# Pairing the 64-row score tiles of an attention + rational-MLP kernel, and moving one PSUM copy from ACT to DVE

## The chip, the cores and the metric

One core of a Trainium2 chip. The metric is the device time of one execution in microseconds (us). The kernel before took 747.16 us, the median of 3 runs (745.7 to 747.44). The engines are called as in the profile: PE is TensorE (its matrix multiplies; PEld is its weight loads), DVE is VectorE, ACT is ScalarE, POOL is GpSimd, SP is SyncE. SBUF is the working memory, PSUM the memory that PE writes its results to.

## The reference

Attention over q, k, v of shape (4, 12, 448, 64), fp32, with capped scores, and a two-layer MLP with a rational activation on its result.

```python
scores = np.matmul(q, k.transpose(0, 1, 3, 2)) / np.sqrt(64)
scores = cap * np.tanh(scores / cap)
attn = np.exp(scores - np.max(scores, axis=-1, keepdims=True))
attn = attn / (np.sum(attn, axis=-1, keepdims=True) + 1e-09)
x = (attn @ v).transpose(0, 2, 1, 3).reshape(1792, 768)
h = x @ w_in                                    # w_in: 768 x 2048
P = a[0] + a[1]*h + a[2]*h**2 + a[3]*h**3
Q = 1.0 + abs(b[0])*abs(h) + abs(b[1])*h**2
out = (P / (Q + 1e-06)) @ w_out                 # w_out: 2048 x 768
```

## The kernel before

The program has two halves: attention (24 pairs of heads, p = 0 to 23), up to about 245 us of the profile, and the MLP. Products are made exact enough by splitting an fp32 operand into a high and a low part: each product is three matmuls (low·high, high·low, high·high).

**Scores (L360).** A pair of heads is worked on together. Its keys are cut into four tiles, n = 0 to 3. Tiles 0 to 2 have 128 keys of each of the two heads, and the head dimension is 64, so the array is used as two halves of 64 rows: head 0 on rows 0 to 63, head 1 on rows 64 to 127. Such a tile is six matmuls of 64 rows by 448 columns (L380), which run two at a time, and it fills both banks of one of the three PSUM buffers PS[0] to PS[2] (448 fp32 columns for each head). Tile 3 holds the last 64 keys of both heads in one product over all 128 rows: three matmuls (L285, `ps`), one bank. A "visit" below is a stretch of PE's order in which only 64-row score matmuls stand. The buffer of tile n of pair p is `(4p + n) % 3` (L365).

**Softmax (L384, L405).** ACT takes tanh in place in PSUM (L392) and exp from PSUM to SBUF (L409), which frees the buffer. DVE splits the result: a cast gives the high part (L416), a subtraction the low part (L417).

**P·V (L446).** For each of the two heads (j = 0, 1): nine matmuls of 66 columns (L285, `pv`) and one in fp32 for the tail (L459, shown as two), all into the one PSUM bank `pv`. Then ACT copies 65 rows x 448 columns of it to SBUF (L470) for either head, which frees the bank for the next head; small DMAs take the denominators and, for j = 1, the result into its place. The P·V of pair p - 1 stands among the score tiles of pair p (L564, L565).

**Preparation (L289).** Two pairs ahead, q and k are transposed on PE (L304 to L310) into `mi`; ACT makes the high parts (L318, L324), DVE the low ones (L319, L327). Pair 1 uses PS[1] and PS[2] for it instead of `mi` (L342 to L343). Besides, pairs 5 to 10 carry the conversion of six weight tiles from 64-bit words (L647 on ACT, L649 to L655 on DVE), the normalisation of finished pairs (L514 on DVE), and pairs 21 to 23 the first splits of x for the MLP (L525 on ACT, L526 on DVE), placed by `XSPLIT` as (pair counted from the end, n).

**What sets the order.** The kernel records every operation with an estimated cost, and a list scheduler (`Plan.flush`, L116) replays them on five engines and emits each engine's order. An engine takes, among what is ready, the operation that stands earliest in the program. The costs fix only the order; on the chip each engine runs its order strictly and waits for semaphores. A 64-row tile is one operation with the cost `SC_NS` = 760 ns (L55, L382). The order in the program is that of the loop at L553: for each pair and n, the scores, the softmax, then preparation, P·V, loads and the rest.

## Time and profile before

| What | Value |
|---|---|
| Median of 3 runs | 747.16 us (745.7 to 747.44) |
| The profiled execution | 744.5 us, of which the span (first to last instruction) is 742.7 us |
| PE busy | 711.1 us (96%) |
| DVE busy | 590.2 us (79%) |
| ACT busy | 529.3 us (71%) |
| POOL busy | 129.6 us (17%) |
| Mean granted clock of TensorE | 0.992 of full speed |

How to read it: "busy" is the time in which at least one instruction of the engine is under way. Matmuls are pipelined: a group's last matmul is still shown as running when the next group begins, so what a group costs PE is the distance from its start to the start of the next group. The same holds, by less, for DVE and ACT. Names such as `ps`, `pv`, `mi` are tiles without their buffer numbers, `arena_f` and `arena_r` the two large SBUF arrays that hold nearly everything.

### The profile page before, as it was taken

The numbers are of one execution on the slowest core, as the hardware profiler recorded it, in microseconds if no ns is written. First come the engines' busy times: TensorE is split into PE (matmuls) and PEld (weight loads), VectorE is DVE, ScalarE is ACT, GpSimd is POOL, SyncE is SP. The second block draws the span as 40 slices with busy tenths as digits, with TensorE's granted clock in tenths as the row PEclk, the third lists the DMA queues.
The fourth block names the chain that finished last, engine by engine and source line by source line (L and its number), as shares of the span: only waits on it lengthen the run. The fifth ranks groups of instructions, "written<-read, shape, count | busy, mean of one in ns | idle before, by whom it ended". The sixth has DMA issues, their size and how long they took to land.

```text
span 742.7 us, 10184 instructions
## 1 busy us (share of the span) xinstructions
PE 711.1 (96%) x3733; PEld 594.1 (80%) x3733; DVE 590.2 (79%) x720; ACT 529.3 (71%) x701; POOL 129.6 (17%) x193
## 2 busy tenths in 40 slices
PE   7999999999999999999799889899999999999996
PEld 4666656665656899989798889789999999999996
DVE  4879989998887689898677767779668878887863
ACT  6999989989898768877676777785674446444560
POOL 3222423422321000221222222120000000000030
PEclk9999999999999999999899999999999999999999
DMA  6668878556244345999899989795420121121065
GB/s 142 157 174 201 214 194 192 129 130 144 54 128 107 91 139 158 251 269 250 216 237 245 240 212 227 165 196 180 140 64 23 43 76 53 43 64 43 1 118 185
DMA packets 92252, 109.48 MB, mean 147 GB/s; under 512 B 50064, under 2 KB 69392, under 8 KB 92192
## 3 DMA queue, kind: packets, MB, share of 16 engines
q1 hardware_dynamic: 78272, 74.77, 34.5%
q0 software_dynamic: 13920, 33.96, 23.5%
q8 instruction: 31, 0.51, 0.3%
q14 instruction: 29, 0.24, 0.1%
HBM read 62.13 MB, written 18.17 MB: 108 GB/s over the span
## 4 chain that ended last, share of the span: by engine, by line
PE 59%; issue 17%; DMA 9%; DVE 6%; ACT 4%; POOL 4%; POOLq 0%; DVEq 0%; ACTq 0%
PE ps L285 20%; PE pv L285 10%; PE ps L751 9%; PE ps L380 5%; PE pv L751 5%; PE mi L751 4%; DMA arena_r<-X 4%; PE pv L459 4%; POOL arena_f L258 3%; DMA arena_f<-arena_f 2%; PE mi L310 1%; DMA arena_f<-dn 1%; ACT ps L392 1%; DMA dn<-arena_f 1%; PE mi L304 1%
## 5 line engine op out<-in xcount | busy, mean ns | idle before, releaser
L285 PE MATMUL ps<-arena_r 128*128 128x448 f32 x1224 | 274.7, 373 | 1.4 <-ACT arena_f L409 1.4
L285 PEld LDWEIGHTS ps<-arena_r 128*128 128x128 f32 x1224 | 229.6, 189 | 28.6 <-issue 5.0
L258 POOL DMA_DIRECT2D arena_f<-arena_f x112 | 79.5, 713 | 456.1 <-ACT arena_f L782 351.5
L751 PE MATMUL ps<-arena_r 128*128 128x384 f32 x672 | 129.7, 339 | 9.3 <-ACT arena_f L782 7.9
L751 PEld LDWEIGHTS ps<-arena_r 128*128 128x128 f32 x672 | 119.3, 190 | 12.8 <-ACT arena_f L782 9.9
L751 PE MATMUL pv<-arena_r 128*128 128x384 f32 x336 | 112.6, 338 | 6.9 <-DMA arena_r<-X 3.7
L751 PE MATMUL mi<-arena_r 128*128 128x384 f32 x336 | 112.7, 338 | 0.6 <-ACT arena_f L782 0.4
L285 PE MATMUL pv<-arena_r 128*66 128x448 f32 x432 | 100.2, 371 | 0.0
L409 ACT ACTIVATE arena_f<-ps,acap 128x896 f32<-128x896 f32 (+1 forms) x96 | 86.2, 920 | 0.4
L720 DVE SCALAR_TENSOR_TENSOR arena_f<-arena_f,bab 128x896 f32<-128x896 f32 x32 | 36.8, 1151 | 58.6 <-ACT arena_f L717 58.5
L285 PEld LDWEIGHTS pv<-arena_r 128*66 128x66 f32 x432 | 56.0, 136 | 31.5 <-issue 5.5
L392 ACT ACTIVATE ps<-ps 128x896 f32<-128x896 f32 (+1 forms) x96 | 76.1, 814 | 5.7 <-PE ps L380 5.2
L417 DVE TENSOR_TENSOR arena_r<-arena_f,arena_r 128x896 fp32r<-128x896 f32 x72 | 77.7, 1082 | 0.9
L751 PEld LDWEIGHTS pv<-arena_r 128*128 128x128 f32 x336 | 63.0, 188 | 10.0 <-ACT arena_f L782 4.9
L671 ACT ACTIVATE arena_r<-X 128x768 fp32r<-128x768 f32 x64 | 54.3, 848 | 20.1 <-DMA X<-w 6.1
L751 PEld LDWEIGHTS mi<-arena_r 128*128 128x128 f32 x336 | 63.1, 188 | 3.2 <-ACT arena_f L782 1.9
L728 ACT CAST arena_r<-arena_f 128x896 fp32r<-128x896 f32 x32 | 30.1, 939 | 46.9 <-DVE arena_f L727 46.9
L380 PE MATMUL ps<-arena_r 64*128 64x448 f32 x432 | 60.6, 392 | 2.1 <-DVE arena_r L319 1.3
L716 ACT ACTIVATE arena_f<-ps,b 128x896 f32<-128x896 f32 x32 | 32.3, 1010 | 40.5 <-PE ps L285 40.5
L380 PEld LDWEIGHTS ps<-arena_r 64*128 64x128 f32 x432 | 35.8, 184 | 28.7 <-issue 17.3
L416 DVE CAST arena_r<-arena_f 128x896 fp32r<-128x896 f32 x72 | 44.1, 618 | 11.2 <-ACT arena_f L409 10.8
L678 DVE SCALAR_TENSOR_TENSOR arena_r<-X,arena_r 128x768 fp32r<-128x768 f32 x48 | 45.7, 951 | 4.0 <-ACT arena_r L671 4.0
(92 smaller groups left out, 901.5 us busy)
## 6 DMA issues: line engine op xcount, KB each, us to landing
arena_f<-arena_f POOLq DMA_DIRECT2D x49, 384.0 KB, 6.9
X<-w SPq DMA_DIRECT2D x38, 384.0 KB, 3.1
arena_f<-in_moe_w_in_dram SPq DMA_DIRECT2D x16, 768.0 KB, 7.1
w<-X SPq DMA_DIRECT2D x32, 384.0 KB, 3.7
arena_f<-in_moe_w_out_dram SPq DMA_DIRECT2D x16, 768.0 KB, 7.8
arena_r<-X POOLq DMA_DIRECT2D x16, 384.0 KB, 8.5
arena_f<-in_q_dram SPq DMA_DIRECT2D x46, 112.0 KB, 4.0
out_dram<-arena_f SPq DMA_DIRECT2D x13, 384.0 KB, 2.3
```

The costliest lines, as they stand in the source:

```text
L258: self.op(eng, (625 if local else 450) if eng == SP else 1050, lambda: e.dma_start(out, in_, **accum), r, w, nbytes=nbytes, **kw)
L285: r = nc.tensor.matmul(out, st, mv, start=(first and y == 0), stop=(last and y == len(ops) - 1))
L380: m = nc.tensor.matmul(self.PS[i][:, j, 0:448], st[r], mv[r], start=y == 0, stop=y == 2)
L392: self.op(ACT, act_ns(448 * w, True), lambda: nc.scalar.activation(ps, ps, AF.Tanh), ["table"], pk)
L409: self.op(ACT, act_ns(448 * w, sk[0][0] == "ps", 1), lambda: nc.scalar.activation(e, src, AF.Exp, scale=acap), sk + ["table"], [ek])
L416: self.op(DVE, dve_ns(448 * w, fast=True), lambda: nc.vector.tensor_copy(eh, e), [ek], [("eh", ih)])
L417: self.op(DVE, dve_ns(448 * w), lambda: nc.vector.tensor_tensor(el, e, f32(eh), ALU.subtract), [ek, ("eh", ih)], [("el", ih)], early=E_EL)
L671: self.op(ACT, act_ns(n, False), lambda: nc.scalar.mul(hl[:, 0], X, c), [xk], [(*hk, 0)])
L678: lambda: nc.vector.scalar_tensor_tensor(hl[:, 1], X, c, f32(hl[:, 0]), ALU.mult, ALU.subtract),
L716: self.op(ACT, act_ns(n, True, 1), lambda: T.activation(Bt, h, AF.Abs, scale=b[:, 0:1]), hk, bk)
L720: self.op(DVE, dve_ns(n, 1), lambda: stt(Bt, C, bab[:, 1:2], Bt, ALU.mult, ALU.add), ck + ["bab"], bk)
L751: r = nc.tensor.matmul(po[n][:, 0:384], st, mv[:, 384 * n:384 * n + 384], start=(y == 0 and x == 0), stop=(y == self.NCH - 1 and x == 2))
```

## The change

- A visit takes two 64-row tiles wherever it can, also of two different pairs. `ORDER` is the order of the tiles in a pair: 0, 1, 3, 2 in even pairs and 0, 1, 2, 3 in odd ones. `GO` says at which step which tiles are issued: in an even pair p, tiles 0 and 1 at step 0, tile 3 at step 2, and tile 2 together with tile 0 of pair p + 1 at step 3; in an odd pair, tiles 1 and 2 at step 1 and tile 3 at step 3. A visit is one operation of the planner with both PSUM buffers as outputs, and all twelve matmuls are emitted in one go. The buffer of a tile follows its place in that order (`bank`).
- The planner's cost of a visit is 610 ns for each tile and 380 ns for the visit, instead of 760 ns for each tile.
- The `pv` result of the second head (j = 1) is copied out of PSUM by DVE (`tensor_copy`) instead of ACT. The first head's stays on ACT.
- `XSPLIT` puts the third split of x one step later (step 3 of the last pair but one) and the sixth two steps later (step 3 of the last pair). Loads that wait for the scores of step n wait for the tile that now stands there.

```diff
--- before.py
+++ after.py
@@ -40,7 +40,7 @@
 HP = 100.0
 HA = 50.0
 HD = 50.0
-XSPLIT = ((-3, 1), (-2, 1), (-2, 2), (-2, 3), (-1, 0), (-1, 1))
+XSPLIT = ((-3, 1), (-2, 1), (-2, 3), (-2, 3), (-1, 0), (-1, 3))
 WARM = 6
 WARM2 = ((3, 4), (0, 0))
 EARLY = (("w_in", 0), ("w_in", 1), ("w_in", 2), ("w_out", 0), ("w_in", 3), ("w_out", 1))
@@ -52,7 +52,8 @@
 E_PR = 20
 E_SC = 0
 E_EL = 0
-SC_NS = 760
+SC_NS = 610
+SC_CHANGE = 380
 OFFR = 3072
 REST = 1
 XOUT_LATER = 3
@@ -357,33 +358,42 @@
                 [("rv", g % 2, 0), ("vh", g % 2, 0)], [("vl", g % 2, 0)])
 
 
-    def scores(self, p, n):
-
-        name, (S, QL) = self.qset(p)
-        nc = self.nc
-        K = lambda s: (name, s)
-        i = (4 * p + n) % 3
-        QH = S[:, 2, 0:448]
-        keys = [K("kl"), K("kh"), K("qh"), K("ql")]
-        w = [("ps", i), ("scores", p, n)]
-        if n == 3:
-            t = slice(384, 512)
-            cost, fn = self.mm([(S[:, 0, t], QH), (S[:, 1, t], QL), (S[:, 1, t], QH)], self.PS[i][:, 0, 0:448], True, True)
+
+    ORDER = ((0, 1, 3, 2), (0, 1, 2, 3))
+    GO = (((0, ((0, 0), (0, 1))), (2, ((0, 3),)), (3, ((0, 2), (1, 0)))), ((1, ((0, 1), (0, 2))), (3, ((0, 3),))))
+
+    def bank(self, p, n):
+        return (4 * p + self.ORDER[p % 2].index(n)) % 3
+
+    def scores(self, tiles):
+
+        nc = self.nc
+        keys, w, todo = [], [], []
+        for p, n in tiles:
+            name, (S, QL) = self.qset(p)
+            i = self.bank(p, n)
+            keys += [(name, s) for s in ("kl", "kh", "qh", "ql")]
+            w += [("ps", i), ("scores", p, n)]
+            QH = S[:, 2, 0:448]
+            t = slice(384, 512) if n == 3 else slice(128 * n, 128 * n + 128)
+            todo.append((self.PS[i], [(S[:, 0, t], QH), (S[:, 1, t], QL), (S[:, 1, t], QH)]))
+        if tiles[0][1] == 3:
+            cost, fn = self.mm(todo[0][1], todo[0][0][:, 0, 0:448], True, True)
             self.op(PE, cost, fn, keys, w, early=E_SC)
             return
-        t = slice(128 * n, 128 * n + 128)
 
         def run():
-            for y, (st, mv) in enumerate(((S[:, 0, t], QH), (S[:, 1, t], QL), (S[:, 1, t], QH))):
-                for j in range(2):
-                    r = slice(64 * j, 64 * j + 64)
-                    m = nc.tensor.matmul(self.PS[i][:, j, 0:448], st[r], mv[r], start=y == 0, stop=y == 2)
+            for po, ops in todo:
+                for y, (st, mv) in enumerate(ops):
+                    for j in range(2):
+                        r = slice(64 * j, 64 * j + 64)
+                        m = nc.tensor.matmul(po[:, j, 0:448], st[r], mv[r], start=y == 0, stop=y == 2)
             return m
-        self.op(PE, SC_NS, run, keys, w, early=E_SC)
+        self.op(PE, SC_NS * len(tiles) + SC_CHANGE, run, keys, w, early=E_SC)
 
     def softmax(self, p, n):
         nc = self.nc
-        i = (4 * p + n) % 3
+        i = self.bank(p, n)
         w = 2 if n < 3 else 1
         ps = self.PS[i][:, 0:w, 0:448]
         pk = [("ps", i)]
@@ -467,7 +477,10 @@
         E = self.U[iu] if j == 0 else self.EB[ib]
         ek = [("u0", iu), ("u1", iu)] if j == 0 else [("eb", ib)]
         sk = [("u1", iu)] if j == 0 else ek
-        self.op(ACT, act_ns(448, True), lambda: nc.scalar.copy(E[0:65], po[0:65, 0:448]), ["pv"], ek, early=E_EV)
+        if j == 0:
+            self.op(ACT, act_ns(448, True), lambda: nc.scalar.copy(E[0:65], po[0:65, 0:448]), ["pv"], ek, early=E_EV)
+        else:
+            self.op(DVE, dve_ns(448), lambda: nc.vector.tensor_copy(E[0:65], po[0:65, 0:448]), ["pv"], ek, early=E_EV)
         h = 3 * j + p % 3
 
         q = SP if self.last_norm(k) else POOL
@@ -552,8 +565,11 @@
 
         for p in range(P1):
             for n in range(4):
-                self.scores(p, n)
-                self.softmax(p, n)
+                for at, tiles in self.GO[p % 2]:
+                    if at == n:
+                        self.scores([(p + d, x) for d, x in tiles])
+                tile = self.ORDER[p % 2][n]
+                self.softmax(p, tile)
                 if n == (0 if self.bounded else 3) and p + 2 < P1:
                     self.prep_qk(p + 2)
                 if not self.bounded:
@@ -566,13 +582,14 @@
                 if n == 2 and p % 2 == 1 and p + 1 < P1:
                     self.prep_v((p + 1) // 2)
                 if n == 3 and p % 2 == 0:
-                    self.load32(p // 2 + 1, [("scores", p, n)])
+                    self.load32(p // 2 + 1, [("scores", p, tile)])
                 step = 4 * (p % 2) + n
                 if step < 5:
-                    self.load(p // 2 + 2, [("scores", p, n)], step, 5)
-                self.early_w(p, n)
-                if self.bounded and (p - P1, n) in XSPLIT:
-                    self.split_x(0, XSPLIT.index((p - P1, n)))
+                    self.load(p // 2 + 2, [("scores", p, tile)], step, 5)
+                self.early_w(p, n, tile)
+                for kc, at in enumerate(XSPLIT if self.bounded else ()):
+                    if at == (p - P1, n):
+                        self.split_x(0, kc)
                 if todo and n % 2:
                     t = todo.pop(0)
                     if t is not None:
@@ -584,14 +601,14 @@
             self.split_x(0, kc)
         return [t for t in todo if t is not None]
 
-    def early_w(self, p, n):
+    def early_w(self, p, n, tile):
 
         if not (self.bounded and self.wide):
             return
         for x, (which, f) in enumerate(EARLY):
             at = EARLY_AT + EARLY_STEP * x
             if (p, n) == (at, 1):
-                self.load_w(0, f, which, [("scores", p, n)], "A")
+                self.load_w(0, f, which, [("scores", p, tile)], "A")
             if (p, n) == (at + 1, 0):
                 self.convert_w(0, f, which)
                 del self.wslot[(0, f, which)]
```

## Rows read from the trace of the kernel before

**Rows 1.** Stretches of attention: start:end width, then busy us (xinstructions) of PE, PEld, DVE, ACT, POOL, PEclk, DMA share, GB/s.

```profile
20.00:60.00 40.00, 39.34 (x225) 25.15 (x224) 32.96 (x47) 37.20 (x55) 10.89 (x19) 1.00 0.67 168
60.00:160.00 100.00, 98.24 (x534) 60.37 (x533) 94.39 (x136) 95.77 (x138) 34.04 (x50) 1.00 0.72 178
160.00:240.00 80.00, 78.65 (x417) 48.43 (x415) 66.19 (x91) 70.95 (x100) 21.81 (x36) 1.00 0.45 110
```

**Rows 2.** The longest of PE's waits, 20 to 240 us: us in total, times, longest.

```profile
PE mi L310 <- DVE arena_r L319: 2.4, 2, 1.8
```

**Rows 3.** Timeline of PE around a visit of one tile: start us, us, what, count.

```profile
151.22 0.91 PE L459 MATMUL pv<-arena_f 128*66 128x448 f32 x2
151.97 0.55 PE L310 MATMUL mi<-ident,arena_f 112*128 112x112 f32 x4
...
163.60 0.92 PE L459 MATMUL pv<-arena_f 128*66 128x448 f32 x2
164.45 0.87 PE L380 MATMUL ps<-arena_r 64*128 64x448 f32 x6
165.25 0.88 PE L285 MATMUL ps<-arena_r 128*128 128x448 f32 x3
165.97 1.39 PE L285 MATMUL pv<-arena_r 128*66 128x448 f32 x6
```

**Rows 4.** Timeline of PE around a visit of two tiles.

```profile
104.60 1.49 PE L380 MATMUL ps<-arena_r 64*128 64x448 f32 x12
106.02 1.43 PE L285 MATMUL pv<-arena_r 128*66 128x448 f32 x6
...
107.28 0.77 PE L285 MATMUL ps<-arena_r 128*128 128x448 f32 x3
107.89 0.37 PE L285 MATMUL pv<-arena_r 128*66 128x448 f32 x1
```

**Rows 5.** Timeline of PE: the first and the last visit.

```profile
9.38 1.25 PE L380 MATMUL ps<-arena_r 64*128 64x448 f32 x6
...
225.15 1.60 PE L380 MATMUL ps<-arena_r 64*128 64x448 f32 x12
```

**Rows 6.** Timeline of DVE where nothing waits.

```profile
149.81 0.68 DVE L319 TENSOR_TENSOR arena_r<-mi,arena_r 128x512 fp32r<-128x512 f32 x1
150.41 0.61 DVE L514 TENSOR_TENSOR arena_f<-arena_f 128x448 f32<-128x448 f32 x1
150.94 0.61 DVE L416 CAST arena_r<-arena_f 128x896 fp32r<-128x896 f32 x1
151.47 0.61 DVE L514 TENSOR_TENSOR arena_f<-arena_f 128x448 f32<-128x448 f32 x1
```

**Rows 7.** Groups by form, 60 to 160 us, and DVE's longest wait there.

```profile
L470 ACT COPY arena_f<-pv 65x448 f32<-65x448 f32 x21 | 11.2, 534 | 1.2 <-PE pv L459 0.9
...
DVE arena_f L514 <- DMA arena_f<-dn: 3.1, 1, 3.1
```

**Rows 8.** Timeline of PE and ACT: a visit and the ACT work on its result.

```profile
160.53 0.88 PE L380 MATMUL ps<-arena_r 64*128 64x448 f32 x6
...
161.45 0.90 ACT L392 ACTIVATE ps<-ps 128x896 f32<-128x896 f32 x1 [0.23 <-PE ps L380]
```

**Rows 9.** Waits of PE's weight loads, 20 to 240 us.

```profile
PEld ps L380 <- ACT arena_f L409: 3.0, 7, 0.7
```

**Rows 10.** Timeline of ACT and DVE at the start.

```profile
10.68 0.90 ACT L392 ACTIVATE ps<-ps 128x896 f32<-128x896 f32 x1 [1.49 <-PE ps L380]
13.77 0.90 ACT L392 ACTIVATE ps<-ps 128x896 f32<-128x896 f32 x1 [0.26 <-PE ps L380]
...
12.12 0.69 DVE L319 TENSOR_TENSOR arena_r<-ps,arena_r 128x512 fp32r<-128x512 f32 x1 [2.21 <-ACT arena_r L318]
```

**Rows 11.** Timeline of DVE and PE at the end of attention.

```profile
230.95 1.08 DVE L526 TENSOR_TENSOR arena_r<-arena_f,arena_r 128x896 fp32r<-128x896 f32 x1
...
234.97 2.95 PE L285 MATMUL ps<-arena_r 128*128 128x448 f32 x12
```


## The prediction

> **What bounds the kernel now.** I read the page first: PE is busy for 96% of the span, so the question in attention is whether PE waits or works. The stretches of attention [rows 1] show PE busy for 216 of 220 us between 20 and 240 us, at a granted clock of 1.00, and the longest entry of PE's waits there is 2.4 us in all [rows 2]. So PE, in the order given to it, sets the pace, and what shortens PE's own work shortens the run, until another engine takes over. The reader is to see in the same rows how near the others are: from 60 to 160 us DVE is busy for 94.39 us of 100 and ACT for 95.77; from 160 to 240 us DVE for 66.19 of 80.
>
> Then the timeline, to price a visit. A group costs PE the distance to the next group's start. Before a visit, the fp32 pair of P·V takes 0.85 us (163.60 to 164.45), where ahead of other work it takes 0.75 (151.22 to 151.97): entering costs 0.10 [rows 3]. A visit of one tile lasts 0.80 us (164.45 to 165.25) [rows 3], one of two tiles 1.42 (104.60 to 106.02) [rows 4], so a tile is worth 0.62 and the visit itself 0.18. The three full-height matmuls behind a visit take 0.72 us (165.25 to 165.97) [rows 3], elsewhere 0.61 (107.28 to 107.89) [rows 4]: leaving costs 0.11. **A visit costs 0.39 us over its matmuls**, whether it holds one tile or two.
>
> From the first to the last visit [rows 5] the timeline has 60 of them for 72 tiles, 48 of one tile and 12 that the planner's order already made double.
>
> **The change part by part.** (1) Visits. `GO` makes three visits of two tiles for every two pairs, 36 in all; the twelve matmuls are one operation, so nothing can come between them. 24 visits go: 24 x 0.39 = **9.4 us less on PE**. Matmuls are neither added nor removed. The order of the tiles is on PE's path, so all of it counts where PE is the bound.
>
> (2) The copy of j = 1. 24 copies leave ACT, 0.53 us each [rows 7], some 12.7 us; since PE sets the pace, ACT's relief by itself is worth 0. DVE gets 24 copies of 448 columns out of PSUM. The trace has no DVE copy from PSUM. Back to back, DVE takes 0.53 us from one start to the next for 448 columns with two SBUF operands (150.41 to 150.94), 0.60 for 512 columns with one operand in PSUM (149.81 to 150.41), the same per column, and 0.53 for a cast of 896 columns within SBUF (150.94 to 151.47), half as much per column [rows 6]. Bounds: 0.27 and 0.60. I take 0.53, by the row that reads PSUM. The Trainium skill, "VectorE: DVE Perf Modes", section "Why PSUM operands drop a tier", says that DVE's doubled rate for fp32 needs both SBUF read ports and that an operand in PSUM has only one; no DVE copy out of PSUM is in this trace to confirm it. By that rule the copy goes at the single rate and the sum below stands; at the doubled rate the next term would be 1.2 us instead of 4.0.
>
> Where does DVE have room? Between 60 and 160 us there are 21 `pv` copies [rows 7], so 10.5 pairs; half of the copies move: 10.5 x 0.53 = 5.6 us. DVE's 94.39 [rows 1] become 100.0. PE's saving in this stretch is 26 visits (counted there) less 10.5 x 1.5, about 10, at 0.39: 4.0 us, which would cut the stretch to 96.0. DVE doesn't fit into that; the stretch stays at 100, and **4.0 us of the 9.4 are given back**. In front of and behind it DVE idles for 7 and 14 us [rows 1], and 13.5 copies add 7.2, so there the copies are hidden by idle time and cost nothing; without that cover they'd cost their 7.2. Bounds of this term: 0 (the lag is carried past 160 us, into the idle 14) and 9.6 (DVE's idle 5.6 us stay, among them the 3.1 us for one DMA of the normalisation [rows 7]). Behind a copy that waits for P·V on DVE stand the casts and subtractions that the next P·V needs; ACT's queue had the same wait before, for every head.
>
> (3) Two PSUM buffers at once. A visit now needs two of three buffers free, so PE reaches ACT's exp more often. From a visit's start to tanh on its result it takes 0.92 us (160.53 to 161.45) [rows 8]; ACT holds one tile meanwhile instead of two. In the trace of before, seven weight loads of score tiles waited for exp, 0.43 us each (3.0 in all) [rows 9]. Bounds: 0, and 0.43 for each of 36 visits, 15.5. Taken: as often as before, 7, in addition only one or two more, **0.5 us**, since ACT is relieved of 0.53 us in each pair and P·V can stand between. A gain is excluded: a wait for two is never shorter than for one.
>
> (4) The start. The first visit takes tiles 0 and 1 of pair 0, and PS[1], which holds the transposed k of pair 1 until DVE's subtraction ends at 12.81 (12.12 + 0.69); tanh of tile 0 ran at 10.68 and that of tile 1 at 13.77 [rows 10]. At worst the first tanh slips to 13.77, 3.1 us. At best nothing, since the transposes no longer stand behind a visit, and ACT does its two copies for pair 1 earlier. Taken **0.7 us**, nearer to the low end: by 13.77 ACT had to do the same copies anyway.
>
> (5) Edits with one answer. The sixth split of x ends at 232.03 (230.95 + 1.08) and the first layer starts at 234.97 [rows 11]; two steps later it would end at about 236, and the products of the other five stand ahead of those that need it: 0, and at worst 1. The loads that follow a tile's scores are issued by SP and POOL at most one tile's turn earlier or later, with a mean DMA share of 0.72 [rows 1] and two pairs of lead: 0. The MLP's order and transfers hang on the end of attention and move with it: 0. The planner's new prices only choose the order.
>
> **Sum**: -9.4 + 4.0 + 0.5 + 0.7 = -4.2 us. The profiled execution took 744.5 us, so 740.3; it lay 2.66 us under the median of 747.16, and against that median the forecast is **743.0 us**.
>
> **The rivals.** *DVE is elastic.* Its lag is carried into the idle time behind 160 us, and term 2 is 0: -8.2, 739.0 us. For it: 14 us idle there. Against it: the order is fixed, and P·V waits for the subtractions. Chance 0.18.
>
> *DVE takes all.* Its 5.6 idle us between 60 and 160 stay, for they are waits for exp and for a DMA: term 2 is 9.6, the sum +1.4, 748.6 us, within what can't be told from no change. For it: DVE is in front already. Against: PE's waits for DVE are but 2.4 us. Chance 0.20.
>
> *PSUM becomes the bound*, the case on the other side. At each visit PE stands still until exp has freed the second buffer, with the whole P·V behind it. If half of the 36 visits wait 0.43 us [rows 9], that is 7.7 us instead of 0.5: +3.0, 750.2 us; if all do, 757.9. It decides from (4.2 + 0.5) / 36 = 0.13 us a visit for break-even, 0.19 for a measurable loss. For it: 3 buffers, pairs of 2. Against: the 12 double visits of before ran without such waits in rows 4. Beside this stands the Trainium skill, "TensorEngine Tiling (Array Packing)", section "Gotcha 1: PSUM Pressure": row tiling raises the pressure on PSUM, as different row tiles write different banks. That agrees with a tile filling both banks of a buffer; no row here shows it as a loss. Chance 0.20.
>
> That the change doesn't do what it says is possible only in part: the groups of twelve are written out, but fewer than 24 visits would go if I miscounted those of before. Under 0.02, within the main case.
>
> **How the numbers follow.** Forecast 0.42, elastic 0.18, DVE takes all 0.20, PSUM 0.20. A measurement can tell about 0.3%, 2.24 us: faster means under 744.92. The forecast's own spread (the start and the price of a copy, some 2 us) puts 0.34 of its 0.42 there and the rest within; with the elastic case 0.52. Same: 0.08 and DVE's case, 0.28. Slower 0.20. The range, 738 to 751, takes in three cases and the lower half of the PSUM case, and leaves out its upper half and a little below the elastic case. The forecast with the elastic case alone would be 738 to 746.
>
> **What would show it.** 36 groups of twelve L380 matmuls on PE, each 1.42 us to the next group; PE's excess gone by 9 us in all; DVE near 10 tenths between 60 and 160 us, with copies from `pv` of 0.5 to 0.6 us; the last P·V 4 us earlier. If PE's waits for exp ahead of L380 pass 5 us, the PSUM rival holds; if PE's waits for DVE's L417 or for the new copy grow by 5 us or more in the middle stretch, DVE takes all. I'd be wrong at the root if a visit of two tiles cost more than 1.42 us, or if the MLP's part changed its length.

## The result: slower by 1.1%, in the middle of attention

Four runs of the changed kernel took 753.96 to 755.62 us, median 754.82; four of the kernel before, beside them, 744.86 to 747.44, median 746.43. The ratio is **1.011 [1.0084, 1.0137]**: some 8 us slower, where 4.2 us faster was forecast, and 3.8 us above the range. The profiled execution took 754.62 us with a span of 752.8, against 744.5 and 742.7 before: 10.1 us of span to find.

Steps of the same work are compared first. The product that ends the second head of a pair (the fp32 pair of P·V, L459 before, L469 after) is a mark that both kernels have 24 times. For pairs 0, 3, 14 and 23 it stands at 25.6, 55.1, 159.3 and 243.4 us before and at 27.6, 56.4, 170.0 and 254.1 after. So the start grew by 2.0 us, pairs 1 to 3 fell from 29.5 to 28.8, **pairs 4 to 14 grew from 104.2 to 113.6**, pairs 15 to 23 stayed at 84.1, and from the last mark to the end it is 499.3 and then 498.7.

The stretches of the three engines in those windows, before (columns: length, then busy us and count of PE, its weight loads, DVE, ACT, POOL; granted clock, DMA share, GB/s):

```profile
55.10:159.30 104.20, 102.44 (x563) 63.48 (x562) 98.29 (x141) 99.89 (x145) 35.96 (x54) 1.00 0.72 179
159.30:243.40 84.10, 82.75 (x434) 51.13 (x433) 66.81 (x92) 71.90 (x102) 21.81 (x36) 1.00 0.45 109
```

The same windows of the changed kernel, and below them its 60 to 160 us, for [rows 1]:

```profile
56.40:170.00 113.60, 102.04 (x553) 64.00 (x552) 107.11 (x155) 95.43 (x133) 42.67 (x58) 0.98 0.70 175
170.00:254.10 84.10, 81.60 (x439) 52.28 (x438) 70.32 (x100) 69.24 (x95) 24.04 (x36) 1.00 0.40 96
...
60.00:160.00 100.00, 90.71 (x498) 56.79 (x496) 94.97 (x138) 85.82 (x121) 37.28 (x49) 1.00 0.71 179
```

PE stands idle for 1.8 us of the middle part before (104.20 less 102.44) and for 11.6 after. DVE's share of it is the same, 94.3% (98.29 of 104.20, 107.11 of 113.60): the part grew as DVE's work did. That work grew by 8.8 us, of which 6.7 are the 11 new copies and 1.9 two weight splits more, which the new order has here. The groups of DVE in 56.4 to 170 us (busy us, mean ns of one, idle before):

```profile
L483 DVE COPY arena_f<-pv 65x448 f32<-65x448 f32 x11 | 6.7, 609 | 0.5 <-DMA arena_f<-arena_f 0.5
L695 DVE SCALAR_TENSOR_TENSOR arena_r<-X,arena_r 128x768 fp32r<-128x768 f32 x4 | 3.8, 940 | 0.0
```

What PE waits for between 20 and 240 us, the view of [rows 2], sums to 3.8 us before. After (us in total, times, longest):

```profile
PE pv L286 <- DVE arena_f L483: 7.0, 8, 2.2
PE mi L311 <- DVE arena_r L320: 6.1, 8, 1.2
PE pv L286 <- ACT arena_f L481: 0.8, 2, 0.6
PE ps L286 <- ACT arena_f L419: 0.2, 1, 0.2
```

That is over 14 us, and it is not for the score buffers that a visit needs. The first line is P·V of a head, which waits until the head before has been copied out of `pv`, a single buffer. The second is the transposes of q (L311), which wait until DVE has read the transposed k out of `mi` (the subtraction, L320): a single buffer too.

The price of a visit came out as forecast. Two rows of PE's timeline (start, us, what, count), from the start of a visit of two to that of the next group:

```profile
107.00 1.50 PE L390 MATMUL ps<-arena_r 64*128 64x448 f32 x12
108.42 1.84 PE L286 MATMUL pv<-arena_r 128*66 128x448 f32 x8
```

It is 1.42 us. To see whether the 24 visits were saved, I added up PE's timeline from the mark of pair 0 to that of pair 23: each distance from one matmul's start to the next, less what that form takes in an unbroken run. Excess into and out of a visit is its overhead; an excess above 0.35 us anywhere is a wait; the rest is small change. The columns leave some 0.5 us over that this count doesn't place.

| pair 0 to pair 23 | length | visits | their overhead | waits | small change |
|---|---|---|---|---|---|
| before | 217.8 | 55 | 16.4 | 3.4 | 9.7 |
| after | 226.5 | 33 | 8.9 | 18.4 | 11.4 |
| difference | +8.7 | -22 | **-7.5** | **+15.0** | +1.7 |

So the saving is there, 7.5 us where 22 x 0.39 = 8.6 was due, and waits of twice its size came with it. With the start (+2.0) and the end (-0.6) that is the span's 10.1 us.

How a wait of the first kind comes about, on PE's timeline from 66 to 72 us (in brackets: idle before, and what ended it):

```profile
66.72 0.91 PE L469 MATMUL pv<-arena_f 128*66 128x448 f32 x2
67.57 1.50 PE L390 MATMUL ps<-arena_r 64*128 64x448 f32 x12
69.34 0.60 PE L311 MATMUL mi<-ident,arena_f 112*128 112x112 f32 x4 [0.28 <-DVE arena_r L320]
69.72 0.86 PE L286 MATMUL ps<-arena_r 128*128 128x448 f32 x3
70.88 1.43 PE L286 MATMUL pv<-arena_r 128*66 128x448 f32 x6 [0.29 <-DVE arena_f L483]
```

and on DVE's timeline of the same time:

```profile
66.54 1.08 DVE L427 TENSOR_TENSOR arena_r<-arena_f,arena_r 128x896 fp32r<-128x896 f32 x1
67.54 0.61 DVE L527 TENSOR_TENSOR arena_f<-arena_f 128x448 f32<-128x448 f32 x1
68.08 0.61 DVE L426 CAST arena_r<-arena_f 128x896 fp32r<-128x896 f32 x1
68.61 0.68 DVE L320 TENSOR_TENSOR arena_r<-mi,arena_r 128x512 fp32r<-128x512 f32 x1
69.22 1.07 DVE L427 TENSOR_TENSOR arena_r<-arena_f,arena_r 128x896 fp32r<-128x896 f32 x1
70.21 0.61 DVE L483 COPY arena_f<-pv 65x448 f32<-65x448 f32 x1
70.75 0.61 DVE L527 TENSOR_TENSOR arena_f<-arena_f 128x448 f32<-128x448 f32 x1
```

P·V's last product ends at about 67.6 us, and the copy of its result could begin. DVE has no pause, but four instructions stand in its queue ahead of the copy, which begins 2.6 us later, at 70.21. PE meanwhile does a visit, four transposes and three full-height matmuls, runs out, and stands. The subtraction at 68.61, which frees `mi`, is late in the same queue. A visit stood in this gap, and the copy came late all the same.

The longest of these waits, 2.21 us, is of another make. DVE's timeline, then PE's, then the stretch behind it:

```profile
159.44 0.63 DVE L527 TENSOR_TENSOR arena_f<-arena_f 128x448 f32<-128x448 f32 x1 [0.90 <-DMA arena_f<-dn]
160.55 0.62 DVE L483 COPY arena_f<-pv 65x448 f32<-65x448 f32 x1 [0.49 <-DMA arena_f<-arena_f]
```

```profile
161.22 1.43 PE L286 MATMUL pv<-arena_r 128*66 128x448 f32 x6 [2.21 <-DVE arena_f L483]
162.59 2.37 PE L390 MATMUL ps<-arena_r 64*128 64x448 f32 x12
164.89 1.01 PE L311 MATMUL mi<-ident,arena_f 112*128 112x112 f32 x4
```

```profile
163.00:166.00 3.00, 3.00 (x17) 2.27 (x14) 3.00 (x5) 0.97 (x2) 0.41 (x1) 0.50 0.46 90
```

Here DVE itself stood: 0.90 us for the broadcast of the sums, and 0.49 us for the transfer that empties the buffer that the copy writes, `EB`, of which there is one. Soon after PE's wait the granted clock of TensorE fell to 0.50, the lower of its two levels (1.2 instead of 2.4 GHz), for 3.4 us: the visit at 162.59 takes 2.30 us to the next group, where others take 1.42. That is what the 0.98 in the window of pairs 4 to 14 means. It costs up to 1.7 us (half of 3.4, an estimate) of the 9.4 by which that part grew; before, the part has no such stretch.

Where the copy stands back to back with what follows (70.21 to 70.75), it costs 0.54 us, and a cast of 896 columns within SBUF 0.53 (68.08 to 68.61). The Trainium skill, "VectorE: DVE Perf Modes", section "Why PSUM operands drop a tier", says that an operand in PSUM loses the doubled rate; these two rows agree, 448 columns from PSUM costing what 896 do within SBUF.

ACT was relieved of its 24 copies, and turned the time into waiting for PE: `ps` L402 from PE, the tanh, grew in the list of ACT's waits from 3.5 us (L392 before) to 17.4 between 20 and 240 us:

```profile
ACT ps L402 <- PE ps L390: 17.4, 18, 2.8
ACT arena_r L325 <- PE mi L311: 7.4, 9, 2.0
```

### The profile page after: what moved, and what is told of

Its sections match the earlier page's. It is cut to its first block, busy times and chain, and to the rows that moved or that the text cites. A ratio compares the mean times of both kernels' runs of the same rounds, so it can differ in the third digit from the quotient of the medians.

```text
span 752.8 us, 10182 instructions
## 1 busy us (share of the span) xinstructions
PE 711.1 (94%) x3733; PEld 596.3 (79%) x3733; DVE 603.1 (80%) x744; ACT 519.7 (69%) x677; POOL 136.1 (18%) x193
## 4 chain that ended last, share of the span: by engine, by line
PE 54%; issue 18%; DMA 13%; ACT 5%; POOL 5%; DVE 5%; SPq 1%; POOLq 0%; ACTq 0%; DVEq 0%
PE ps L286 20%; DMA arena_f<-arena_f 10%; PE ps L768 10%; PE pv L286 7%; PE pv L768 5%; PE mi L768 5%; POOL arena_f L259 3%; PE ps L390 3%; PE pv L469 3%; DVE arena_r L427 1%; DMA arena_f<-dn 1%; ACT arena_f L799 1%; POOL arena_r L259 1%; DMA arena_r<-X 1%; ACT arena_f L419 1%
## 5 line engine op out<-in xcount | busy, mean ns | idle before, releaser
L259 POOL DMA_DIRECT2D arena_f<-arena_f x112 | 87.1, 783 | 446.1 <-ACT arena_f L799 327.7
L768 PE MATMUL ps<-arena_r 128*128 128x384 f32 x672 | 130.6, 342 | 11.4 <-ACT arena_f L799 11.4
L768 PEld LDWEIGHTS ps<-arena_r 128*128 128x128 f32 x672 | 119.9, 192 | 16.6 <-ACT arena_f L799 15.8
L768 PE MATMUL pv<-arena_r 128*128 128x384 f32 x336 | 112.5, 337 | 3.6 <-DMA arena_r<-X 2.5
L402 ACT ACTIVATE ps<-ps 128x896 f32<-128x896 f32 (+1 forms) x96 | 76.3, 815 | 17.7 <-PE ps L390 17.6
L390 PE MATMUL ps<-arena_r 64*128 64x448 f32 x432 | 54.7, 385 | 1.2 <-ACT arena_f L419 1.2
L390 PEld LDWEIGHTS ps<-arena_r 64*128 64x128 f32 x432 | 38.4, 187 | 19.5 <-issue 10.6
```

Of the source, the lines that this page charges most:

```text
L259: self.op(eng, (625 if local else 450) if eng == SP else 1050, lambda: e.dma_start(out, in_, **accum), r, w, nbytes=nbytes, **kw)
L390: m = nc.tensor.matmul(po[:, j, 0:448], st[r], mv[r], start=y == 0, stop=y == 2)
L402: self.op(ACT, act_ns(448 * w, True), lambda: nc.scalar.activation(ps, ps, AF.Tanh), ["table"], pk)
L768: r = nc.tensor.matmul(po[n][:, 0:384], st, mv[:, 384 * n:384 * n + 384], start=(y == 0 and x == 0), stop=(y == self.NCH - 1 and x == 2))
```

## The experiments

18 kernels ran, each beside the kernel before on the same chip. In the table a ratio is to that kernel before (median 745.49 to 746.97 us), with its 95% interval; the part from pair 4 to 14, and visits, overhead and waits from pair 0 to 23, are counted as above on each profiled execution. Labels are explained below it.

| kernel | median us | ratio | pairs 4 to 14 | visits | overhead | waits |
|---|---|---|---|---|---|---|
| before | 746.43 | 1 | 104.1 | 55 | 16.4 | 3.4 |
| after | 754.82 | 1.011 [1.0084, 1.0137] | 113.6 | 33 | 8.9 | 18.4 |
| e1 | 753.78 | 1.0092 [1.0059, 1.0126] | 115.8 | 33 | 8.7 | 21.3 |
| e2 | 748.5 | 1.003 [1.0, 1.0061] | 112.5 | 49 | 14.1 | 7.4 |
| e3 | 750.4 | 1.006 [1.0036, 1.0083] | 109.0 | 33 | 8.1 | 16.6 |
| e4 | 757.28 | 1.0127 [1.0083, 1.0171] | 111.6 | 60 | 16.9 | 9.2 |
| e5 | 743.71 | 0.9963 [0.9941, 0.9986] | 103.6 | 53 | 15.5 | 2.7 |
| e6 | 749.03 | 1.0043 [1.0018, 1.0067] | 104.5 | 50 | 14.4 | 5.9 |
| e7 | 752.06 | 1.0093 [1.006, 1.0125] | 112.8 | 33 | 8.9 | 17.9 |
| e8 | 759.26 | 1.0179 [1.0153, 1.0205] | 115.9 | 33 | 8.3 | 23.5 |
| e9 | 752.51 | 1.0115 [1.0075, 1.0156] | 110.6 | 33 | 9.9 | 14.6 |
| e10 | 749.0 | 1.0037 [1.002, 1.0054] | 110.0 | 33 | 9.1 | 14.3 |
| e11 | 753.56 | 1.0104 [1.0065, 1.0143] | 113.1 | 59 | 16.5 | 8.8 |
| e12 | 753.3 | 1.0077 [1.0037, 1.0116] | 113.9 | 33 | 9.6 | 17.9 |
| e13 | 757.26 | 1.0167 [1.012, 1.0214] | 110.8 | 33 | 9.4 | 14.4 |
| e14 | 750.59 | 1.0055 [1.0018, 1.0093] | 111.1 | 55 | 16.7 | 7.8 |
| e15 | 749.29 | 1.004 [1.0017, 1.0062] | 108.0 | 33 | 9.5 | 11.4 |
| e16 | 749.94 | 1.0056 [1.0035, 1.0077] | 105.8 | 33 | 10.7 | 10.3 |
| e17 | 748.99 | 1.0023 [1.0001, 1.0046] | 111.3 | 33 | 9.4 | 12.5 |
| e18 | 747.02 | 1.0002 [0.9984, 1.0021] | 102.6 | 55 | 16.4 | 1.6 |

The last four columns come from one execution of each kernel, which isn't always a typical one: that of e1 was its slowest (761.93 us), those of e13 and e16 were their fastest (749.59 and 746.04). Nor is a longer middle always lost time: in e2 588 matmuls stand in it, against 563 before, so that it holds work of other pairs too, and pairs 15 to 23 take 79.5 us there instead of 84.1. And stretches of 3.4 us or more at the granted clock of 0.50 fall into the middle of some profiled executions (after, e1, e7, e10 to e14, e17) and not of others, which is worth some 2 us between two rows.

e4, e6 and e12 don't give the reference's result, though only their order differs from kernels that do: in these orders something is read or overwritten at the wrong time, a dependence that the planner's list lacks; which one isn't known. Their times show what an order is worth, and no more.

**The two halves of the change, e1 to e4.** e1 has the visits without the copy on DVE, e2 the copy without the visits. In e1, against the changed kernel:

```
-        if j == 0:
+        if True:
             self.op(ACT, act_ns(448, True), lambda: nc.scalar.copy(E[0:65], po[0:65, 0:448]), ["pv"], ek, early=E_EV)
```

> The changed kernel with both pv copies back on ACT; the 36 paired visits stay. Theory DVE (the copy on DVE holds the single pv bank behind a full DVE queue, and that alone makes the changed kernel slower): PE's 7.0 us of waits for the DVE copy and most of its 6.1 us for the q/k subtraction go, the 9.4 us of visits come through, 737 to 742 us, ratio to the kernel before 0.987 to 0.995. Rival PSUM (two buffers at once starve ACT: its waits for score tiles rose from 5.2 to 17.6 us): still slower than before, ratio 1.005 to 1.015, and ACT's waits for the score matmuls stay at 15 us or more.

e2 is the kernel before with the four lines of the diff at L470 that give j = 1 to DVE, and nothing else.

> The kernel before with the second head's pv copy on DVE, nothing else. Theory DVE: slower by 8 to 18 us, ratio 1.011 to 1.024, with PE's waits for the copy at 5 us or more between 60 and 160 us. Rival PSUM: no change, ratio 0.998 to 1.003. If each part alone is harmless and only both together are slow, ratio below 1.003 here and below 1.0 for the visits alone.

e3 is the changed kernel with the copy on DVE everywhere but in the crowded pairs:

```
-        if j == 0:
+        if j == 0 or 3 < p < 16:
```

> The changed kernel with the second head's copy on ACT for pairs 4 to 15 (the stretch in which DVE also converts weights) and on DVE for the others. Theory DVE saturated in that stretch alone: nearly as fast as with all copies on ACT, within 2 us, as DVE has idle time elsewhere. If the copy is slow wherever it stands (a wait at the head of DVE's queue, not its load): about half way between the changed kernel and the one with all copies on ACT. Rival PSUM: as slow as the changed kernel, within 2 us.

e4 keeps the kernel before and only tells its planner that a visit is dear, as the change does:

```
-SC_NS = 760
+SC_NS = 990
```

> The kernel before with the planner's price of a 64-row tile at 990 ns, what a single visit costs on PE by the profile, instead of 760. If the planner's price matters by itself (it moves the order of P.V, preparation and softmax): 2 to 5 us either way. If the order hardly depends on it: within 1.5 us of the kernel before.

The copy alone costs 0.3% (e2), with an interval that reaches down to nothing; the changed kernel without it in the middle is faster than with it (1.006 against 1.011), and without it anywhere (e1) it should be faster still, but its interval overlaps both. e1 fits neither of its theories: the ratio is the rival's, but ACT's waits for the score matmuls fell to 6.7 us, and the wait for the subtraction that frees `mi` rose to 12.6, of which 6.7 are the one stall of the last section. Nor is it the copy that takes most: with it or without it, no kernel with 33 visits came out faster than before. And e4 changes no instruction and loses 1.3%. An experiment that changes one operation also draws a new order from the planner, and the price of the order is as large as what was to be measured.

**The order by itself, e5 to e9.** The next five vary that one price, in the kernel before (`SC_NS` 740 and 780 for 760) and in the changed one (570, 650 and 470 for 610).

> The kernel before with the planner's price of a 64-row tile at 740 ns instead of 760; the work is the same, only the order of the queues can change. Theory order (the time depends on the one order that the planner happens to give, by several us, and the order of before is a good draw): slower by 3 to 10 us. Theory mechanism (paired visits starve ACT and DVE by themselves): within 1.5 us of the kernel before.

> The same at 780 ns. Theory order: slower by 2 to 10 us, and not by the same as at 740. Theory mechanism: within 1.5 us of the kernel before.

> The changed kernel with a tile at 570 ns in the planner, so that a visit of two costs 1520 as two single tiles did before. Theory order: a time of its own, more than 3 us from the changed kernel, somewhere from 741 to 758 us. Theory mechanism: 753 to 757 us, with 36 visits, and PE's waits ahead of the q transposes and of P.V as in the changed kernel.

> The changed kernel with a tile at 650 ns in the planner (a visit of two at 1680). Theory order: more than 3 us from the changed kernel and from the run at 570, either way. Theory mechanism: 753 to 757 us.

> The changed kernel with a tile at 470 ns in the planner (a visit of two at 1320, 0.82 of what it costs on PE, the share at which the kernel before priced its tiles). So far a lower price went with a shorter time in both kernels (740, 760, 780: 743.7, 746.4, 749.0 us; 570, 610, 650: 752.1, 754.8, 759.3 us). Theory price (a part of the loss is the planner's dearer visit, 1600 against 2 x 760): 744 to 748 us. Theory pairs (the grouping itself costs): 750 us or more. Theory chance of order: anywhere from 744 to 758, off the line of the other three.

At 740, 760, 780 and 990 the kernel before has ratios of 0.9963, 1, 1.0043 and 1.0127; at 470, 570, 610 and 650 the changed kernel has 1.0115, 1.0093, 1.011 and 1.0179. The draw is worth some 0.4% either way, more with a price far off, and **every draw of the changed kernel is slower than the three near draws of the kernel before**. Its slowdown isn't one unlucky order, though a part of it can be. The expectations of e5 were both missed: it came out faster, where slower or the same was expected. It is faster than both kernels, by a constant alone. Its windows:

```profile
55.40:158.90 103.50, 102.73 (x566) 63.76 (x565) 99.19 (x142) 99.61 (x146) 35.95 (x54) 1.00 0.78 188
158.90:242.10 83.20, 81.86 (x430) 50.87 (x428) 65.64 (x91) 71.61 (x101) 22.38 (x36) 1.00 0.41 100
```

PE idles there for 0.8 us of the first and 1.3 of the second: there is next to nothing left to wait for.

**The visits again, from a better draw, e10 and e11.** e10 is e1 at the price of e9:

```
-SC_NS = 610
+SC_NS = 470
...
-        if j == 0:
+        if True:
```

> Both pv copies on ACT, paired visits, a tile at 470 ns in the planner. Theory price: 742 to 747 us, below the kernel with all copies on ACT at 610 (753.8) by 6 or more. Theory pairs: 750 to 755 us.

e11 is the other way round: the changed kernel, copy and tile order and all, with every tile an operation of its own, so that the planner may put work between any two:

```
-    GO = (((0, ((0, 0), (0, 1))), (2, ((0, 3),)), (3, ((0, 2), (1, 0)))), ((1, ((0, 1), (0, 2))), (3, ((0, 3),))))
+    GO = (((0, ((0, 0),)), (1, ((0, 1),)), (2, ((0, 3),)), (3, ((0, 2),))), tuple((x, ((0, x),)) for x in range(4)))
```

> The changed kernel (its tile order, buffers, splits and the copy on DVE) with every 64-row tile as an operation of its own, at 990 ns (610 and 380). Visits rise from 36 to 55 or more, which costs PE 7 us or more. Theory pairs (waiting for two buffers, and bursts of two tiles, cost more than the visits that they save): faster than the changed kernel by 2 us or more in spite of that. Theory price: at 990 ns for each tile slower, 757 us or more. If only visits count: slower by about 7 to 9 us, 762 to 764 us.

At the same price, e10 against e9 is the copy on DVE in a kernel with double visits: 1.0037 [1.002, 1.0054] against 1.0115 [1.0075, 1.0156], so the copy costs some 0.8% there, by the two intervals 0.3 to 1.2. At the price of 610 it is 0.2% (after against e1), by itself 0.3% (e2): it costs some tenths of a per cent, not told better than that. And e10 alone is the visits without the copy: **+0.4% where the 9.4 us would be -1.3%**. The windows of e10 say where they are and where they aren't:

```profile
56.90:166.90 110.00, 101.55 (x557) 64.41 (x556) 103.78 (x146) 100.45 (x146) 32.16 (x56) 0.98 0.72 181
166.90:248.20 81.30, 79.81 (x430) 50.69 (x429) 64.63 (x90) 72.28 (x102) 21.88 (x36) 1.00 0.38 95
```

In pairs 15 to 23, where DVE is busy for 79% (64.63 of 81.30), the part fell from 84.1 to 81.3: 2.8 us, and 20 visits became 12, 8 x 0.39 = 3.1. There the forecast's first term holds, and in e15 to e17 too (81.2, 81.0 and 79.8 us; the 86.0 of e1 hold 3.4 us at the granted clock of 0.50). With the copy on DVE it doesn't: the changed kernel, e3 and e9 take 84.1, 83.8 and 83.8 us for these pairs, though DVE is busy for 82 to 84% only. PE waits there, in e9 from 167.5 to 251.3 us:

```profile
PE pv L286 <- DVE arena_f L483: 2.7, 4, 1.5
```

In pairs 4 to 14, where DVE is busy for 94%, the part grew from 104.1 to 110.0. What PE waits for between 20 and 240 us, e10 and then e11:

```profile
PE mi L311 <- DVE arena_r L320: 7.6, 10, 1.6
PE pv L286 <- ACT arena_f L481: 3.6, 8, 0.8
```

```profile
PE mi L311 <- DVE arena_r L320: 4.9, 5, 2.6
PE pv L286 <- DVE arena_f L483: 2.2, 2, 1.9
PE ps L390 <- ACT arena_f L419: 0.2, 1, 0.2
```

e11 is as slow as the changed kernel (1.0104 against 1.011) with 26 visits more: it pays 7.6 us more overhead (16.5 against 8.9) and 9.6 us less in waits (8.8 against 18.4). Two readings fit this: **a visit covers about as much as it costs PE, or PE doesn't set the pace of the middle**, so that what is saved on it becomes waiting. The middles of e11 and of e3 speak for the second, with DVE as the engine that sets it:

```profile
55.00:168.20 113.20, 107.08 (x569) 64.18 (x568) 106.62 (x155) 98.17 (x136) 38.06 (x55) 0.98 0.71 173
56.00:165.00 109.00, 100.50 (x557) 63.60 (x556) 102.64 (x145) 100.48 (x145) 34.45 (x56) 1.00 0.74 183
```

DVE has the same work in e11 as in the changed kernel (106.62 and 107.11 us), and the middles are as long (113.2 and 113.6). e3 has 4.5 us less of it, with the visits of the changed kernel, and its middle is 4.6 us shorter, of which up to 1.7 may be the clock. In e10 DVE's work there is 5.5 us above that of before, and the part 5.9 us longer.

What is covered can be counted on PE's timeline between the last product of one head's P·V and the first of the next, the time in which `pv` has to be copied out. Of 47 such gaps 43 have a visit in them before, 44 in e11, 23 after and 22 in e10; in the lists of PE's waits P·V waits for a copy never before, for 2.2 us in e11, 7.8 after and 3.6 in e10. For copies on ACT that agrees: the six waits of e10 that pass 0.2 us are all in gaps without a visit. For copies on DVE it doesn't: of the nine after, four have a visit in their gap, as in the example at 70.88 us, and e9 and e13, with a visit in 30 and 32 gaps, wait for 8.3 and 9.8 us. There the copy is late because it stands in DVE's queue.

**Taking the waits away, e12 to e18.** e12 lets the multiplication L527 come later (`XOUT_LATER = 5`), to have less in DVE's queue ahead of the copies.

> The changed kernel with the multiplication by the reciprocal sums put two turns later in the program (XOUT_LATER 5 instead of 3), so that DVE doesn't stand at it until the broadcast DMA has landed. Theory DMA wait in DVE's queue (in the run with both copies on ACT one such wait of 6.9 us stopped PE for 6.7): faster than the changed kernel by 2 to 6 us, and DVE's waits for the DMA from dn under 1 us. Rival: those waits are covered by slack, time within 1.5 us of the changed kernel.

It moved nothing that can be told from the changed kernel (1.0077 [1.0037, 1.0116]); waits 17.9. e13 to e15 have DVE's subtraction read no `mi`, so that the bank comes free with ACT's copy; k's low part is zero in them, and the instruction is as long as before:

```
-        ... nc.vector.tensor_tensor(S[:, 0, :], pk, f32(S[:, 1, :]), ALU.subtract),
-                bk + [K("kh")], [K("kl")], early=E_PR)
+        ... nc.vector.tensor_tensor(S[:, 0, :], f32(S[:, 1, :]), f32(S[:, 1, :]), ALU.subtract),
+                [K("kh")], [K("kl")], early=E_PR)
```

e13 does this to the changed kernel, e14 to the one before, e15 to e10.

> The changed kernel in which the low part of k is taken from the high part alone (it is zero, so the low.high product of the scores adds nothing); DVE does the same amount of work, but the bank mi is free as soon as ACT has copied it. Theory bank (PE waits for mi ahead of the q transposes): PE's excess ahead of them falls from 9 us to 5 or less, time 747 to 751 us. Theory copy (the rest of the loss is the DVE copy's hold on pv): the waits ahead of P.V stay at 12 us or more and the kernel stays slower than before. Rival: the bank doesn't matter, 753 to 756 us.

> The kernel before with the same replacement (low part of k zero). Theory bank: it waits for the bank 2.4 us only, so at most 3 us faster, 743 to 746 us. Rival (the bank costs every kernel the same): as much faster as in the changed kernel.

> Paired visits, both copies on ACT, a tile at 470 ns, low part of k zero. Theory bank: the 9 us of visits come through in good part, 739 to 744 us, faster than the kernel before with the same replacement. Rival (paired visits lose by bursts, wherever the waits fall): 747 us or more, and the waits turn up ahead of P.V or of the scores instead.

e16 is e10 with that subtraction, and the rest of the preparation of q and k, planned earlier (`E_PR` 60 for 20).

> Paired visits, both copies on ACT, a tile at 470 ns, and the copies and subtractions of the preparation 60 instead of 20 places earlier in the planner's order; the computation is whole. Theory bank: DVE's k subtraction comes sooner, 743 to 747 us. Rival: the planner already takes them when they are ready, 748 to 750 us as without it.

e17 is e10, and e18 the kernel before, with only 112 of 448 columns copied out of `pv`, so that the other bank comes free sooner; POOL fills the rest once, ahead of the first pair:

```
-            ... nc.scalar.copy(E[0:65], po[0:65, 0:448]), ["pv"], ek, early=E_EV)
+            ... nc.scalar.copy(E[0:65, 0:112], po[0:65, 0:112]), ["pv"], ek, early=E_EV)
```

> Paired visits, both copies on ACT, a tile at 470 ns, and the copy out of pv takes 112 of the 448 columns (the other 336 are left out; they are set once at the start by POOL). The planner's price and with it the order of all engines stays. The copy holds the bank 0.28 us less. Theory cover (P.V waits for the copy where no visit stands between two chains, 25 of 47 gaps): PE's waits ahead of P.V fall by 4 us or more, and the kernel is faster by 3 to 7 us than without the edit (749.0), 742 to 746 us. Rival (the copy is covered; ACT's queue or DVE's sets the pace): as much faster as the kernel before is by the same edit.

> The kernel before with the same edit of the copy (112 of 448 columns, the others left out). Theory cover: its copies lie beside a visit in 43 of 48 gaps, so at most 1.5 us faster, 745 to 747 us. Rival (ACT's load counts): faster by 3 us or more, as ACT is relieved of 13 us.

Each edit did at its place what it was made for, and the time didn't follow. PE's waits of e13, e15 and e17, in that order:

```profile
PE pv L286 <- DVE arena_f L483: 8.7, 7, 2.6
...
PE mi L311 <- ACT arena_r L319: 0.7, 1, 0.7
```

```profile
PE pv L286 <- ACT arena_f L481: 5.6, 10, 1.1
PE mi L305 <- DVE arena_r L328: 2.9, 5, 1.1
```

```profile
PE mi L311 <- DVE arena_r L320: 9.2, 9, 1.9
PE pv L286 <- ACT arena_f L481: 1.0, 3, 0.5
```

With `mi` free, the wait for L320 (6.1 us after, 7.6 in e10) is gone, and P·V waits instead: 8.7 us in e13, 5.6 in e15. With `pv` copied in a quarter of the columns, P·V's wait is down from 3.6 to 1.0, and the transposes of q wait for 9.2 instead of 7.6. The times are 1.004 (e15) and 1.0023 (e17) against 1.0037 for e10, all within each other's intervals (the middle of e15 is 2.0 us shorter than that of e10, and up to 1.7 of it is the clock, 0.50 for 3.4 us in e10's and nowhere in e15's); e13, whose four runs spread from 749.59 to 760.74 us, is if anything slower than the changed kernel. So neither bank, taken alone, is the cause. Either PE is made to stop at whichever of them comes first, or another engine sets the pace and PE's waits only show it. The kernel before, with a shorter copy, doesn't change either (e18, 1.0002). By the expectations of e17 that speaks for its rival: the cover was to be worth 3 to 7 us in e17, and both kernels moved by less than 0.2%, as they should if ACT's queue or DVE's sets the pace. ACT was relieved as well, its copies taking 0.25 us instead of 0.54, which points to DVE. In e15 too the rival came true: past 747 us, with the waits ahead of P·V.

e16 has the shortest middle of the paired kernels, 105.8 us, and the least waits, 10.3; its median of 749.94 isn't below that of e10.

## Why the prediction was wrong

**Term 1, 9.4 us less on PE: its size was nearly right, its conclusion not.** 60 visits became 36, a visit of two takes 1.42 us as forecast, and 7.5 of the 8.6 us due between pairs 0 and 23 are missing from PE's timeline. The step that failed is the sentence behind the product, "The order of the tiles is on PE's path, so all of it counts where PE is the bound". [rows 1] and [rows 2] show a PE that doesn't wait *in the order that it had*, in which a visit stood in 43 of 47 gaps between two heads' P·V. The 0.80 us of a single visit was also time in which ACT copied `pv` out and DVE got to `mi`, and the change takes half of those covers away. What the runs showed in place of the 9.4 us: 7.5 us of overhead gone and 15.0 us more of waits; in the list of waits 13.1 of 14 us are for DVE's copy out of `pv` and DVE's subtraction from `mi`; and without the copy on DVE a kernel that is 0.4 to 0.9% slower than before (e10, e1) instead of 1.3% faster. That the missing cover is the cause is argued, not shown; a DVE that is as good as full in pairs 4 to 14 explains the same waits. The prediction let DVE bound that stretch only with the copies added, at 100 us, and took the 5.6 us in which DVE waits there for room.

**Term 3, 0.5 us for two PSUM buffers at once, was put at the wrong buffers.** PE's waits for exp came to 1.1 us between 20 and 260 us, 1.4 before, and those of its weight loads for score tiles fell from the 3.0 us of [rows 9] to 1.7, so the score buffers hold. A visit's wait for two buffers cost nothing that can be seen. The prediction had no price for waits at `pv` and `mi`, one buffer each, and all but 0.2 of the 14 us of waits of the list are there. The Trainium skill, "TensorEngine Tiling (Array Packing)", section "Gotcha 1: PSUM Pressure", speaks of the banks that row-tiled matmuls write; by these waits, no loss shows at those banks here.

**Term 2, the copy on DVE: price right, cover wrong.** A copy takes 0.54 us where it is one of a row and 0.61 alone; 0.53 was taken. But the middle was forecast to stay at 100 us, on the ground that DVE would fill its idle 5.6 us, and DVE didn't: its share of the middle is 94.3% in both kernels, and lies between 89 and 97% in all that ran. Much of the rest were waits for the normalisation's transfers, 3.4 of 5.9 us before and 4.4 of 6.5 after, which copies in the same queue don't fill. In front of the middle and behind it the copies were to be hidden by idle time; behind it, in pairs 15 to 23, they took the saving back (83.8 us in e9 against 81.3 in e10), since PE waits for a copy in a queue that is only four fifths full too. In all, the 0.2 to 0.8% that the copies cost can't be told from the term's 4.0 us (0.5%).

**Term 4, the start**, came to 2.0 us where 0.7 was taken, within its bounds of 0 and 3.1. The first tanh, at 10.68 us before [rows 10], of the changed kernel:

```profile
12.69 1.71 ACT L402 ACTIVATE ps<-ps 128x896 f32<-128x896 f32 x2 [0.18 <-PE ps L390]
```

**Term 5** was right: the last part got 0.6 us shorter, and nothing else changed in it.

**The rivals.** "DVE takes all" named the place, and was nearer than the forecast. Its test asked for 5 us more of waits in the middle stretch: those for the new copy are 3.6 us between 60 and 160 us, and 5.9 in pairs 4 to 14, so it is met by the pairs and not by the stretch. It gave 748.6 us, since it let PE keep its saving outside that stretch, and it doesn't explain why e1 and e10 are slow with both copies on ACT. "PSUM becomes the bound" gave 750.2 to 757.9 and has the sign and the size, but by waits for exp at the score tiles, which the rows exclude: that would have been luck. What came is a fourth case: the visits' saving turns into waits for two single buffers, `pv` and `mi`, that ACT and DVE have to empty, and the copies on DVE are paid on top (e9 against e10, and pairs 15 to 23).

**What stays open.** What paces the paired kernels between pairs 4 and 14 isn't settled: freeing either bank moved PE's wait to the other, and both at once wasn't tried. DVE, as the engine that sets the pace there, fits e3, e11, e15 and e17, but no run takes work from DVE in the kernel with both copies on ACT; why DVE has 5.5 us more to do there in e10 than before, with no copy added, is explained in part only (two weight splits, 1.9 us). Nor was a second `EB` tried. Nor can the planner's draw be taken out of any single comparison: e1 and e10 are the same edit at two prices and lie 0.55% apart, and e14, which only takes a wait away from the kernel before, is 0.55% slower than it.

## What to carry to other kernels

Overhead on the engine that sets the pace may be time that others, nearly as busy, need to empty a single buffer: before work is grouped to save it, list the gaps between two uses of each such buffer and what stands in each. Idle time on an engine that takes its queue in order isn't room by itself: what it does between 94% of the time and all of it can be waiting, and a copy that another engine waits for was paid even where DVE was busy for some four fifths of the time (e9 against e10, pairs 15 to 23). And where a planner draws the order, run the kernel at two or three neighbouring prices before a per cent is put down to an edit; here the price alone gave the one version that beats both kernels (e5, 0.9963).

## What the runs showed beside that

In the profiled execution of e1 (761.93 us; its other three took 751.39 to 755.2) one transfer held up every engine. The two broadcasts of the sums for the normalisation took 10.4 us from issue to landing (their median) in this stretch, where the same group's median was 5.3 over 20 to 240 us, while the mean DMA share was above 1.0; the second landed at 132.2 us, 13.9 us after its issue. Windows, then DVE, PE and the DMA issues of 110 to 135 us (KB each, median us to landing):

```profile
124.00:128.00 4.00, 3.24 (x17) 1.97 (x16) 1.31 (x2) 3.54 (x6) 0.52 (x1) 1.00 1.09 176
128.00:132.00 4.00, 1.98 (x14) 1.05 (x12) 0.00 (x0) 0.00 (x0) 0.00 (x0) 1.00 1.05 197
134.70:141.50 6.80, 4.82 (x14) 3.10 (x15) 6.80 (x9) 5.46 (x8) 1.05 (x2) 0.50 0.08 17
```

```profile
132.26 1.16 DVE L527 TENSOR_TENSOR arena_f<-arena_f 128x448 f32<-128x448 f32 x2 [6.94 <-issue]
```

```profile
136.68 1.01 PE L311 MATMUL mi<-ident,arena_f 112*128 112x112 f32 x4 [6.70 <-DVE arena_r L320]
```

```profile
arena_f<-dn POOLq DMA_DIRECT2D x2, 336.0 KB, 10.4
```

DVE stood for 6.9 us at the head of its queue with a multiplication that needs the broadcast, the subtraction that frees `mi` behind it, and PE lost 6.7 us at the next transposes. The view names no releaser for DVE's wait ("issue"); that it was the broadcast follows from its landing, 0.1 us ahead of the multiplication. Behind PE's stop the granted clock was 0.50 for 6.8 us, so that the stall cost more than its own length. An order is good or bad in the middle stretch by such meetings too, which no view of the instructions' own durations shows.
